# A two-part start, a moved weight queue and a re-made order for the first couples of an attention-plus-FFN kernel

## Chip, cores, metric

One core of one Trainium2 chip. The metric is the device time of one execution in microseconds (us). Every time below is from runs in the fast state unless it is called a single look. In single looks, which have one execution of each kernel, the state is unknown.

## The reference, cut to what matters

```python
q, k, v: float32 (8, 12, 448, 64)         # batch, heads, sequence, head dim
w_a, w_b: float64 (768, 1536); w_out: float64 (1536, 768)   # no astype: 8 bytes each
q_n = q / sqrt(mean(q*q) + 1e-6) * g_q     # the same for k
attn = softmax(q_n @ k_n.T / 8) @ v
x = attn.transpose(0, 2, 1, 3).reshape(3584, 768)
out = ((x @ w_a) * (x @ w_b)) @ w_out
```

Two things matter here. The q of a head must be squared, summed and rooted before its first score. And the weights arrive as 64-bit numbers (the "words" below), which the kernel has to fetch (1.5 MB for each of 18 pieces), round, combine into seven sums and store again ("kept") before the FFN can use them. That is done during the first twelve couples of the attention. A couple is four heads of one batch element; there are 24, numbered from 0.

## The kernel before

The kernel does not write its instructions in a fixed order. It describes them as operations with an engine, an estimated duration, a priority (a lower key goes first), what they read and write, and how many KB they load. `Plan.run` then simulates the engines and emits the operations in the order in which they would start. The emitted order is final: where ScalarE stood 3.51 us at a square in before's trace (86.13 us), the exponentials emitted behind it came after it (86.99 us), and TensorE waited 2.50 us for them.

```python
class Plan:
    TURN = 0.18
    LANES = 8
    RATE, LANDING = 300.0, 2.0      # belief: KB per us, and us from the last byte to usable
    LAG = 0.1                       # belief: from the end on one engine to the start on another
    ...
    def run(self):
        ...                         # the candidate that can start first, ties by key
                if ops[x][7]:       # a transfer: all of them share one modelled DMA
                    dma = max(dma, t) + ops[x][7] / self.RATE
                    end[x] = dma + self.LANDING
        ...
        for _, n in order:
            if ops[n][3] is not None:
                ops[n][3]()         # emitted in this order
```

The loads of q, k and v are issued by SyncE, one buffer each for q and k. The square is an operation of ScalarE, the sum of VectorE, the root of GpSimd:

```python
        def loads(p, nm):
            ...
            def emit():
                x = ld.tile(..., tag=nm, bufs=2 if nm == "v" else 1)
                for w in range(2):
                    nc.sync.dma_start(x[low_high[w]], pair.rearrange(...))
            op("SP", 0.8 if nm != "k" else 1.4, p - (1.8 if nm == "v" else 2.0), emit, [], [t], new=[t],
               kb=460 if nm != "k" else 800, dmas=2)
        ...
        def squares(s, nm):
                    nc.scalar.activation(t, flat, AF.Square)
                op("ACT", 1.07, key, square, [f"{nm}{p}"], [sq], new=[sq])
                op("DVE", 1.1, key, <sum of the squares>, [sq], [f"{ms}/{nm}"])
```

The words are issued by ScalarE, gated by how far the scores have come, and the rounded sums are stored from ScalarE's queue too:

```python
        LOADS = "ACT"
        KEEPS = "ACT"
        ...
                op(LOADS, 0.45, key - 0.75, load, after, [f"{row}/{part}"], kb=768)   # two per piece
        ...
            op(KEEPS, 0.45, key, keep, ..., kb=1376)
        ...
        GATES = [0, 2, 4, 4, 5, 5, 7, 7, 8, 8, 10, 10, 16, 18, 21, 21, 27, 32]
        seq = [15, 13, 16, 12, 14, 0, 1, 2, 3, 4, 5, 6, 7, 8, 9, 10, 11, 17]
```

The exponentials of the scores are ScalarE's as well. So one engine, in one fixed order, does the squares (which wait for loads), the exponentials (for which TensorE waits) and part of the rounding.

## Time and profile before

| | before |
|---|---|
| time, median of 4 runs | 1550.0 us (1547.28 to 1551.54) |
| span of the profiled execution | 1548.6 us |
| TensorE busy in it | 1506.9 us |
| TensorE idle: start and tail / first scores to 130 us / 130 to 250 / 250 to 1000 / later | 11.0 / 9.9 / 8.8 / 7.9 / 4.1 us |
| ScalarE waiting for q or k at a square, 13 to 245 us | 9.9 us |

The idle times are counted from the trace's matmul records; "start and tail" is what is left of span minus busy time. The three largest waits of TensorE over the whole run, in the view of who waited for whom (total us, times, longest):

```profile
PE sc L515 <- ACT ET L521: 10.6, 20, 1.3
PE o L537 <- ACT ET L521: 6.9, 8, 2.5
PE sc L515 <- ACT qkT L501: 6.0, 10, 1.2
```

All three are waits for ScalarE: twice for an exponential (ET), once for the copy of the transposed q (qkT). None is longer than 2.5 us. The start and the longest waits are shown in the prediction.

### The profile page before, as it was taken

What the parts mean: (1) busy time and instruction counts of PE and PEld (TensorE: products, weight loads), DVE (VectorE), ACT (ScalarE), POOL (GpSimd) and SP (SyncE); (2) the same over time, 40 slices, a digit from 0 to 9 for tenths busy, and PEclk for the clock granted to TensorE, in tenths of its full rate; (3) what the DMA queues carried; (4) which work ended last, traced back from release to release, by engine and by line L of the source; (5) the groups of instructions that cost most, each with busy time, mean ns of one, the idle gap of its engine ahead of it and who ended that gap; (6) DMA issues with size and microseconds to landing.
All of it is one profiled execution on the core that took longest, in us unless ns stands there. A gap on an engine that the chain in (4) does not pass through costs nothing.

```text
span 1548.6 us, 18051 instructions
## 1 busy us (share of the span) xinstructions
PE 1506.9 (97%) x6996; PEld 822.6 (53%) x6996; DVE 813.7 (53%) x1179; ACT 400.7 (26%) x654; POOL 314.1 (20%) x166
## 2 busy tenths in 40 slices
PE   8988999999999999999999999999999999999998
PEld 5553345555444555555444455555547855555796
DVE  5877869888786412222587543222237622222583
ACT  6767661111567100000445500000041000000000
POOL 3426432111345200011244300000111001000000
PEclk9999999999999999999999999999999999999999
DMA  9897445644445542212345456121226742222343
GB/s 269 240 268 199 97 108 178 218 163 175 143 118 128 150 146 76 103 71 107 102 110 152 114 159 199 72 107 71 95 83 206 247 159 100 79 82 91 111 140 110
DMA packets 128866, 214.74 MB, mean 139 GB/s; under 512 B 57860, under 2 KB 108292, under 8 KB 119044
## 3 DMA queue, kind: packets, MB, share of 16 engines
q1 hardware_dynamic: 100708, 160.02, 35.0%
q10 hardware_dynamic: 28064, 53.48, 9.9%
q8 instruction: 57, 0.93, 0.2%
q14 instruction: 37, 0.30, 0.1%
HBM read 169.08 MB, written 44.21 MB: 138 GB/s over the span
## 4 chain that ended last, share of the span: by engine, by line
PE 82%; DMA 7%; DVE 5%; ACT 3%; issue 1%; POOL 1%; SPq 1%; ACTq 0%; DVEq 0%; POOLq 0%
PE pq L1003 48%; PE po L726 16%; PE sc L515 5%; PE o L537 4%; DMA q_sb<-in_q_dram 2%; PE g L901 2%; PE a L901 2%; ACT ET L521 2%; PE pt L494 2%; DMA rec<-inv 1%; PE b L901 1%; PE su L573 1%; PE e L901 1%; PE d L901 1%; DMA lraw<-in_moe_w_b_dram 1%
## 5 line engine op out<-in xcount | busy, mean ns | idle before, releaser
L1003 PE MATMUL pq<-x,st 128*128 128x448 f32 x2016 | 763.5, 540 | 0.9 <-ACT rec L586 0.9
L1003 PEld LDWEIGHTS pq<-x,st 128*128 128x128 f32 x2016 | 381.2, 190 | 379.5 <-issue 371.2
L521 ACT ACTIVATE ET<-sc,ms 128x448 f32<-128x448 f32 x336 | 191.7, 633 | 92.2 <-PE sc L515 65.6
L515 PE MATMUL sc<-qkT 64*64 64x448 f32 x1344 | 177.2, 544 | 18.0 <-ACT ET L521 10.6
L537 PE MATMUL o<-ET,v_sb 64*64 64x448 f32 x1344 | 187.2, 545 | 7.5 <-ACT ET L521 6.9
L464 POOL TENSOR_TENSOR ms<-ms,expo 128x14 f32<-128x14 f32 x48 | 145.6, 3037 | 188.3 <-DVE ms L462 187.6
L1051 POOL TENSOR_TENSOR hT<-hT,t 128x448 f32<-128x448 f32 x24 | 28.4, 1185 | 744.7 <-DVE t L1049 742.5
L726 PE MATMUL po<-st,hT 128*128 128x384 f32 x504 | 166.4, 487 | 0.0
L726 PEld LDWEIGHTS po<-st,hT 128*128 128x128 f32 x504 | 95.0, 190 | 67.9 <-issue 3.9
L551 POOL TENSOR_TENSOR sum<-sum,ET 128x896 f32<-128x896 f32 x38 | 81.4, 2141 | 139.1 <-ACT ET L521 97.0
L1025 ACT COPY hT<-pq 128x448 f32<-128x448 f32 x24 | 12.8, 532 | 372.9 <-PE pq L1003 372.9
L515 PEld LDWEIGHTS sc<-qkT 64*64 64x64 f32 x1344 | 58.1, 132 | 95.2 <-issue 34.8
L537 PEld LDWEIGHTS o<-ET,v_sb 64*64 64x64 f32 x1344 | 60.2, 132 | 87.9 <-ACT ET L521 42.2
L726 PE MATMUL po<-st,fin 128*128 128x384 f32 x264 | 89.9, 490 | 0.0
L551 DVE TENSOR_TENSOR sum<-sum,ET 128x896 f32<-128x896 f32 x57 | 62.8, 1101 | 26.6 <-POOL sum L551 19.4
L726 PEld LDWEIGHTS po<-st,fin 128*128 128x128 f32 x264 | 49.1, 190 | 39.0 <-issue 7.0
L1063 POOL TENSOR_TENSOR hT<-hT,t 128x448 f32<-128x448 f32 x48 | 58.5, 1219 | 53.7 <-DVE t L1060 45.5
L458 DVE TENSOR_REDUCE ms<-sq 128x14 f32<-128x896 f32 x48 | 51.8, 1079 | 27.7 <-ACT sq L456 27.5
L1056 DVE TENSOR_TENSOR hT<-U,pq 128x448 f32<-128x448 f32 x48 | 29.8, 621 | 66.5 <-PE pq L1003 66.5
L746 DVE TENSOR_TENSOR o_sb<-fin,po 128x384 f32<-128x384 f32 x36 | 20.0, 554 | 80.2 <-PE po L726 72.4
L1060 DVE TENSOR_TENSOR t<-U,pq 128x448 f32<-128x448 f32 x48 | 29.7, 619 | 59.6 <-PE pq L1003 57.3
L1028 ACT COPY t<-pq 128x448 f32<-128x448 f32 x24 | 12.8, 533 | 176.0 <-PE pq L1003 176.0
(117 smaller groups left out, 1297.0 us busy)
## 6 DMA issues: line engine op xcount, KB each, us to landing
st<-kept SPq DMA_DIRECT2D x36, 1344.0 KB
st<-kept_o SPq DMA_DIRECT2D x28, 1152.0 KB
kept<-st ACTq DMA_DIRECT2D x12, 1344.0 KB
ti<-kept_t SPq DMA_DIRECT2D x48, 288.0 KB
q_sb<-in_q_dram SPq DMA_DIRECT2D x48, 224.0 KB
k_sb<-in_k_dram SPq DMA_DIRECT2D x48, 224.0 KB
v_sb<-in_v_dram SPq DMA_DIRECT2D x48, 224.0 KB
rec<-inv SPq DMA_DIRECT2D x48, 224.0 KB
```

The source lines that it names most:

```text
L458: op("DVE", 1.1, key, lambda: nc.vector.tensor_reduce(rs[p][:, s], xs["sq", nm, p], AX, ALU.add), [sq], [f"{ms}/{nm}"])
L464: lambda: nc.gpsimd.tensor_tensor(msf(), msf(), expo[:, 0:2 * NT * (b - a)], ALU.pow), [], names)
L494: nc.tensor.transpose(t[:, j * P:(j + 1) * P], x[:, j].rearrange("p h d -> p (h d)"), ident)
L515: nc.tensor.matmul(t[low_high[w], e, 0:S], lhsT=qkTs[p][low_high[e], 1, j * P + w * D:j * P + (w + 1) * D], rhs=qkTs[p][low_high[e], 0, w ...
L521: nc.scalar.activation(E[:, e], scs[p, j][:, e, 0:S], AF.Exp, scale=rs[p][:, 1, 2 * j + e:2 * j + e + 1])
L537: nc.tensor.matmul(os_[p][low_high[e], w, 0:S], lhsT=xs["v", p][low_high[w], e, j * D:(j + 1) * D], rhs=ETs[p, j][low_high[w], e], start=( ...
L551: two[e].tensor_tensor(sums[p], sums[p] if j > 1 else ETs[p, 0], ETs[p, j], ALU.add)
L726: nc.tensor.matmul(held["po"][:, 0:HALF], lhsT=a[0]()[:, c], rhs=sts[beta, 12 + place_of[f]][:, c], start=(c == 0), stop=(c == MH - 1))
L901: nc.tensor.matmul(held[bank], lhsT=x()[:, c], rhs=y(c), start=(start and c == 0), stop=(stop and c == MI - 1), skip_group_check=True)
L1003: nc.tensor.matmul(banks[bank][:, 0:S], lhsT=sts[at][:, f, c * P:(c + 1) * P], rhs=quads[x][:, c], start=(start and c == 0), stop=(stop an ...
L1056: take("DVE", 0.68, lambda bank=bank, i=i, n=n: V.tensor_tensor(C(i, n), held["U"], PS(bank), ALU.add), [f"p{ident_}.{bank}", U], [hp[i]])
L1063: lambda i=i, n=n, nm=nm: two[TIMES].tensor_tensor(C(i, n), C(i, n), held[nm], ALU.mult), [t], [hp[i]],
```

## The change

The intent: shorten the chain before the first scores by doing the first couple's q in two parts (four columns and three) and keep TensorE busy meanwhile with a sixth warm-up step; take the issues of the words off ScalarE; and let the plan make the order of the lead with other delays, meant to be closer to the chip's (the plan's belief, which no run here measures: a result reaches TensorE 0.22 us after it is done and the other engines after 0.05; DMA at 330 KB per us with 3 us landing). The core of the diff:

```diff
-    RATE, LANDING = 300.0, 2.0
-    LAG = 0.1
+    RATE, LANDING = 330.0, 3.0
+    LAG, LAG_PE = 0.05, 0.22
...
-        WARM = 5
+        WARM = 6
-        LOADS = "ACT"
+        LOADS = "SP"
-        ADD_UP = [None, 'DVE', 'POOL', 'DVE', 'POOL', 'DVE', 'DVE']
+        ADD_UP = [None, 'DVE', 'DVE', 'POOL', 'DVE', 'DVE', 'POOL']
...
-                op(LOADS, 0.45, key - 0.75, load, after, [f"{row}/{part}"], kb=768)
+                op(LOADS, 0.45, key - 0.25, load, after, [f"{row}/{part}"], kb=768)
...
+        FIRST = "q", 0
+        PARTS = slice(0, NT // 2 + 1), slice(NT // 2 + 1, NT)
+
+        def begin_first():            # second half of q 0, issued at once on ScalarE's queue
+            x = xs[FIRST] = ld.tile([P, 2, NT * D], FP32, tag="q", name="q_sb", bufs=1)
+            nc.scalar.dma_start(x[low_high[1]], q[0, 2:4].rearrange("h (p j) d -> p h (j d)", j=NT))
+
+        def prepare_first():          # square, sum, scale, root, product: each for c in range(2)
+            ...
+                op("ACT", 0.1 + 0.13 * n, key, square, ["q0"], [f"{sq}/{c}"], ...)
+                op("DVE", 0.1 + 0.145 * n, key, <sum>, [f"{sq}/{c}"], [f"{ms}/q{c}"])
+                op("POOL", 0.4 + 0.32 * n, key, <root>, [], [f"{ms}/q{c}"])
+                op("DVE", 0.1 + 0.145 * n, key, apply, [f"{ms}/q{c}", "q0"], [f"{qn}/{c}"], ...)
...                                    # k's roots, transposes and copy of q of couple 0: in two parts too
-            op("SP", 0.8, p - 0.0, spread_out, [t], [few], new=[few], kb=20, dmas=2)
+            op("SP", 0.8, p - 1.0, spread_out, [t], [few], new=[few], kb=20, dmas=2)
...                                    # the other three steps of the reciprocals likewise
-        GATES = [0, 2, 4, 4, 5, 5, 7, 7, 8, 8, 10, 10, 16, 18, 21, 21, 27, 32]
-        seq = [15, 13, 16, 12, 14, 0, 1, 2, 3, 4, 5, 6, 7, 8, 9, 10, 11, 17]
+        GATES = [0, 2, 5, 7, 10, 13, 14, 15, 19, 22, 24, 24, 26, 29, 30, 32, 40, 42]
+        seq = [12, 13, 15, 14, 16, 0, 1, 2, 3, 4, 5, 6, 7, 8, 9, 10, 11, 17]
-                    factors(n, x * 0.45 + 1.0, x < 2, [after])
+                    factors(n, x * 0.55 + 0.25, x < 1, [after])
```

No line of the diff orders the lead directly. The order comes out of the plan, so every constant above can move every instruction.

More of the change, by code (lines that the diff above doesn't have):

```diff
@@ L154, in run @@
                 for u in users.get(x, ()):
-                    ready[u] = max(ready[u], end[x] + (self.LAG if ops[u][0] != e else 0.0))
+                    ready[u] = max(ready[u], end[x] + ((self.LAG if e != "PE" else self.LAG_PE) if ops[u][0] != e else 0.0))
                     need[u] -= 1
@@ L429, in emit @@
             def emit():
-                x = ld.tile([P, NT, 2, D] if nm == "k" else [P, 2, NT * D], FP32, tag=nm, name=nm + "_sb", bufs=2 if nm == "v" else 1)
-                for w in range(2):
+                if (nm, p) == FIRST:
+                    x = xs.pop(FIRST)
+                else:
+                    x = ld.tile([P, NT, 2, D] if nm == "k" else [P, 2, NT * D], FP32, tag=nm, name=nm + "_sb", bufs=2 if nm == "v" else 1)
+                for w in range(1 if (nm, p) == FIRST else 2):
                     pair = src[b, h0 + 2 * w:h0 + 2 * w + 2]
@@ L435, in emit @@
                 xs[nm, p] = x
-            op("SP", 0.8 if nm != "k" else 1.4, p - (1.8 if nm == "v" else 2.0), emit, [], [t], new=[t],
-               kb=460 if nm != "k" else 800, dmas=2)
+            op("SP", 1.6 if (nm, p) == FIRST else 0.8 if nm != "k" else 1.4, p - (1.8 if nm == "v" else 2.0), emit, [], [t], new=[t],
+               kb=460 if nm != "k" else 800, dmas=1 if (nm, p) == FIRST else 2)
+        FIRST = "q", 0
[3 more added lines that the diff above has]
+            nc.scalar.dma_start(x[low_high[1]], q[0, 2:4].rearrange("h (p j) d -> p h (j d)", j=NT))
@@ new lines, in prepare_first, with begin, square, apply @@
+        def prepare_first():
+            ms, key, sq = tile_of("ms0", "ms", 3), -NORM, tile_of("sqq0", "sq", 1)
+            cut = lambda x, c: x.rearrange("p h (j d) -> p h j d", d=D)[:, :, PARTS[c]]
+            def begin():
+                rs[0] = wk.tile([P, 2, 2 * NT], FP32, tag="ms", name="ms", bufs=3)
+            op(None, 0.0, key, begin, [], [f"{ms}/q0", f"{ms}/q1", f"{ms}/k"], new=[ms])
+            qn = tile_of("qn0", "qn", 1)
+            for c in range(2):
+                n = PARTS[c].stop - PARTS[c].start
+                r = lambda c=c: rs[0][:, 0].rearrange("p (h j) -> p h j", j=NT)[:, :, PARTS[c]]
+                def square(c=c):
+                    if c == 0:
+                        xs["sq", "q", 0] = wk.tile([P, 2 * NT, D], FP32, tag="sq", name="sq")
+                    nc.scalar.activation(xs["sq", "q", 0].rearrange("p (h j) d -> p h j d", j=NT)[:, :, PARTS[c]], cut(xs[FIRST], c), AF.Square)
+                def apply(c=c, r=r, n=n):
+                    if c == 0:
+                        qns[0] = wk.tile([P, NT, 2, D], FP32, tag="qn", name="qn")
+                    nc.vector.tensor_tensor(
+                        qns[0].rearrange("p j h d -> p h j d")[:, :, PARTS[c]], cut(xs[FIRST], c),
+                        r().rearrange("p h j -> p h j ()").to_broadcast([P, 2, n, D]), ALU.mult)
+                op("ACT", 0.1 + 0.13 * n, key, square, ["q0"], [f"{sq}/{c}"], new=[sq] if c == 0 else [])
+                op("DVE", 0.1 + 0.145 * n, key, lambda c=c, r=r: nc.vector.tensor_reduce(
+                    r(), xs["sq", "q", 0].rearrange("p (h j) d -> p h j d", j=NT)[:, :, PARTS[c]], AX, ALU.add), [f"{sq}/{c}"], [f"{ms}/q{c}"])
+                op("DVE", 0.2, key, lambda r=r: nc.vector.tensor_scalar(r(), r(), 1.0 / D, 1e-6, ALU.mult, ALU.add), [], [f"{ms}/q{c}"])
+                op("POOL", 0.4 + 0.32 * n, key, lambda c=c, r=r, n=n: nc.gpsimd.tensor_tensor(
+                    r(), r(), expo[:, 0:2 * n].rearrange("p (h j) -> p h j", h=2), ALU.pow), [], [f"{ms}/q{c}"])
+                op("DVE", 0.1 + 0.145 * n, key, apply, [f"{ms}/q{c}", "q0"], [f"{qn}/{c}"], new=[qn] if c == 0 else [], lock=True)
@@ L439, in normalize @@
         def normalize(p):
-            ms, key = tile_of(f"ms{p}", "ms", 3), p - NORM
+            ms, key = f"ms{p}", p - NORM
             def begin():
                 rs[p] = wk.tile([P, 2, 2 * NT], FP32, tag="ms", name="ms", bufs=3)
-            op(None, 0.0, key, begin, [], [f"{ms}/q", f"{ms}/k"], new=[ms])
+            if p:
+                tile_of(ms, "ms", 3)
+                op(None, 0.0, key, begin, [], [f"{ms}/q", f"{ms}/k"], new=[ms])
+            else:
+                prepare_first()
@@ L472, in apply @@
                     ALU.mult)
-            squares(0, "q")
-            if p < APART:
-                roots(0, 1, [f"{ms}/q"])
+            if p:
+                squares(0, "q")
+                if p < APART:
+                    roots(0, 1, [f"{ms}/q"])
             squares(1, "k")
-            if p < APART:
+            if p == 0:
+                op("DVE", 0.2, key, lambda: nc.vector.tensor_scalar(rs[0][:, 1], rs[0][:, 1], 1.0 / D, 1e-6, ALU.mult, ALU.add), [],
+                   [f"{ms}/k", f"{ms}/k0", f"{ms}/k1"])
+                for c in range(2):
+                    r = lambda c=c: rs[0][:, 1, 2 * PARTS[c].start:2 * PARTS[c].stop]
+                    n = 2 * (PARTS[c].stop - PARTS[c].start)
+                    op("POOL", 0.4 + 0.16 * n, key, lambda r=r, n=n: nc.gpsimd.tensor_tensor(r(), r(), expo[:, 0:n], ALU.pow), [], [f"{ms}/k{c}"])
+            elif p < APART:
                 roots(1, 2, [f"{ms}/k"])
@@ L480, in normalize @@
                 roots(0, 2, [f"{ms}/q", f"{ms}/k"])
-            qn = tile_of(f"qn{p}", "qn", 1)
-            op("DVE", 1.15, key, apply, [f"{ms}/q", f"q{p}"], [qn], new=[qn], lock=True)
+            if p:
+                qn = tile_of(f"qn{p}", "qn", 1)
+                op("DVE", 1.15, key, apply, [f"{ms}/q", f"q{p}"], [qn], new=[qn], lock=True)
         def transposes(p):
@@ L503, in take, with turn_part, take_part @@
                                              AF.Copy, scale=gain[:, 0:1])
+                if (nm, p) == FIRST:
+                    for c in range(2):
+                        m = PARTS[c].stop - PARTS[c].start
+                        def turn_part(c=c):
+                            if c == 0:
+                                pts[0, 0] = ps_s.tile([P, 2 * 512], FP32, tag="sc", name="pt")
+                            for j in range(NT)[PARTS[c]]:
+                                nc.tensor.transpose(pts[0, 0][:, j * P:(j + 1) * P], qns[0][:, j].rearrange("p h d -> p (h d)"), ident)
+                        def take_part(c=c):
+                            nc.scalar.activation(qkTs[0][:, 0].rearrange("p (w j t) -> p w j t", w=2, j=NT)[:, :, PARTS[c]],
+                                                 pts[0, 0][:, 0:2 * S].rearrange("p (j w t) -> p w j t", w=2, j=NT)[:, :, PARTS[c]],
+                                                 AF.Copy, scale=gain[:, 0:1])
+                        op("PE", 0.11 * m, key, turn_part, [f"qn0/{c}"], [f"{pt}/{c}"], new=[pt] if c == 0 else [], mode="full")
+                        op("ACT", 0.1 + 0.145 * m, key, take_part, [f"{pt}/{c}", "gain"], [f"{qkT}/0"])
+                    continue
                 op("PE", 0.75, key, turn, [f"{nm}{p}" if n else f"qn{p}", f"half{p - 1}"], [pt], new=[pt], mode="full")
@@ L524, in scores @@
                mode="quad")
-            op("ACT", 1.12, p, exps, [sc, f"ms{p}/k"], [E], new=[E])
+            op("ACT", 1.12, p, exps, [sc, f"ms{p}/k" if p else f"ms0/k{int(j >= PARTS[1].start)}"], [E], new=[E])
         def values(p, j):
@@ L604, in invert @@
                 op("ACT", 0.55, p - 0.5, lambda w=w: move(w), [f"su{p}.{w}" if p < WIDE else f"su{p}"], [t], new=[t] if w == 0 else [])
-            op("SP", 0.8, p - 0.0, spread_out, [t], [few], new=[few], kb=20, dmas=2)
-            op("DVE", 0.3, p - 0.0, lambda: nc.vector.reciprocal(fews[0], fews[0]), [], [few])
-            op("SP", 0.4, p - 0.0, leave, [few], [f"inv{p}"], kb=20)
-            op("SP", 1.0, p - 0.0, come_back, [f"inv{p}"], [t], kb=460, dmas=2)
+            op("SP", 0.8, p - 1.0, spread_out, [t], [few], new=[few], kb=20, dmas=2)
+            op("DVE", 0.3, p - 1.0, lambda: nc.vector.reciprocal(fews[0], fews[0]), [], [few])
+            op("SP", 0.4, p - 1.0, leave, [few], [f"inv{p}"], kb=20)
+            op("SP", 1.0, p - 1.0, come_back, [f"inv{p}"], [t], kb=460, dmas=2)
         def quad(b, half):
@@ L1157, in fast_body @@
         with tc.manual_schedule():
+            begin_first()
             setup()
```

## The prediction

> **What bounds the kernel now.** I read the page first, then TensorE's busy time by stretches, then who TensorE waited for, then the first 16 us in order of time, and last the order of instructions of both programs on each engine.
>
> ```profile
> span 1548.6 us, 18051 instructions
> PE 1506.9 (97%) x6996; PEld 822.6 (53%) x6996; DVE 813.7 (53%) x1179; ACT 400.7 (26%) x654; POOL 314.1 (20%) x166
> ```
>
> TensorE is the bound: 1506.9 of 1548.6 us. The change takes no matrix product away (only the warm-up gains four), so all that it can win is TensorE's idle time, 1548.6 - 1506.9 = 41.7 us, and a part of its warm-up. Faster by 2% would need 31 us of these 41.7. The stretches say where the idle time lies (second column: length, then TensorE's busy time):
>
> ```profile
> 14.00:130.00 116.00, 106.09 (x1003) 63.66 (x999) 96.23 (x111) 83.95 (x129) 41.59 (x12) 1.00 0.95 265
> 130.00:245.00 115.00, 106.21 (x738) 46.71 (x731) 84.50 (x104) 72.29 (x117) 61.56 (x27) 1.00 0.51 132
> ```
>
> In the lead (the first twelve couples, up to 245 us) TensorE is idle for 9.9 + 8.8 = 18.7 us. Before 13.65 us it has no product of the attention at all. After 245 us some 16 us remain, over half of that in the last 450 us, at the products of the output and the last stores, whose order the change hardly touches. In the first stretch DMA is busy for 95%, VectorE for 83% and ScalarE for 72%, beside the time it spends issuing loads.
>
> The start, in order of time:
>
> ```profile
> 0.74 1.44 SPq L433 DMA_DIRECT2D q_sb<-in_q_dram  x2
> 1.36 5.66 PE L1094 MATMUL warm<-ident 128*128 128x128 f32 x32 [1.36 <-POOL ident masks.py:199]
> 5.30 0.95 ACT L456 ACTIVATE sq<-q_sb 128x896 f32<-128x896 f32 x1 [2.85 <-DMA q_sb<-in_q_dram]
> 6.28 1.08 DVE L458 TENSOR_REDUCE ms<-sq 128x14 f32<-128x896 f32 x1 [6.28 <-ACT sq L456]
> 7.73 5.15 POOL L464 TENSOR_TENSOR ms<-ms,expo 128x14 f32<-128x14 f32 x2 [6.27 <-DVE ms L462]
> ...
> 9.28 0.91 ACT L499 COPY qkT<-pt 128x896 f32<-128x896 f32 x1
> ...
> 10.36 1.09 DVE L468 TENSOR_TENSOR qn<-q_sb,ms 128x896 f32<-128x896 f32 x1 [0.18 <-DMA v_sb<-in_v_dram]
> 11.51 0.98 PE L494 MATMUL pt<-ident,qn 128*128 128x128 f32 x7 [1.24 <-DVE qn L468]
> 12.59 1.01 ACT L501 ACTIVATE qkT<-pt,gain 128x896 f32<-128x896 f32 x1 [2.40 <-PE pt L494]
> 13.65 1.73 PE L515 MATMUL sc<-qkT 64*64 64x448 f32 x16 [1.16 <-ACT qkT L501]
> ```
>
> It is one chain with nothing beside it: q lands at 5.30, then square, sum, root (half of 5.15), product, seven transposes, copy, and the first scores at 13.65: 8.35 us from the landing.
>
> Two of the waits in the lead:
>
> ```profile
> 74.10 1.73 PE L515 MATMUL sc<-qkT 64*64 64x448 f32 x16 [1.14 <-ACT qkT L501]
> 87.66 1.12 PE L537 MATMUL o<-ET,v_sb 64*64 64x448 f32 x5 [2.50 <-ACT ET L521]
> 86.13 0.95 ACT L456 ACTIVATE sq<-q_sb 128x896 f32<-128x896 f32 x1 [3.51 <-DMA q_sb<-in_q_dram]
> ```
>
> The first is a couple's boundary, where nothing stands between the transposes and the scores that need their copy: 1.14 us. The other two belong together: ScalarE stood 3.51 us at a square whose q had not landed, the exponentials behind it came late, and TensorE paid 2.50 us. This is an order made with a wrong idea of when q lands.
>
> [...] the warm-up's matmul records come at 6 to 7 per us until about 5 us and 10 per us after it. [...] in the trace the first transposes do start after all of the first 16 warm-up matmuls. [...] Here an issue of words costs ScalarE's queue 0.34 to 0.45 us, and DMA is near its limit in the first 130 us, so moving the words to the other queue should give ScalarE this time, not bandwidth.
>
> **The change, part by part.**
>
> 1. *q's second half is issued from ScalarE's queue.* The two issues of 1.44 us now stand beside each other, so the second starts some 0.75 us earlier, and k and the gains behind it too. I put q's landing at 4.6 and the gains' at 7.2 (before: 7.87).
>
> 2. *q in parts of four and three.* ScalarE's 448 elements take 532 ns and 896 take 951, so 0.11 + 0.94 per thousand: squares of 0.59 and 0.47. VectorE by the same reasoning: sums of 0.67 and 0.53, products of 0.68 and 0.55. A root of 14 took 2.57; I take 0.4 fixed: 1.64 and 1.33. Then: first sum 5.2 to 5.9, scaled at 6.1, second sum and its scaling to 6.8. In the new order VectorE does the gains next (0.35 + 0.21 + 0.14 and gaps), which land at 7.2: until 8.05. The roots run 6.15 to 7.8 and to 9.1. First product 8.1 to 8.8; then the sum of k (1.08) to 9.9; second product to 10.5. Three transposes with their drain to 11.15, copy of three columns to 11.75, scores at **11.8**. The other way into the scores is TensorE's own: its order is now 24 warm-up matmuls, gain, k's transposes, q's. The first 16 end at 7.0, eight more at 0.2 us each at 8.6; gain and k's transposes until 9.6; k's copy (0.91) to 10.55; the copies of q's two parts (0.59 + 0.47) to 11.75: the same 11.8. So the first scores come 13.65 - 11.8 = **1.85 us** earlier. The four added matmuls are paid beside q's chain.
>
> 3. *Words on the other queue.* Seven factors are loaded in the first 130 us, two issues each: 14 x 0.42 = 5.9 us that ScalarE's queue no longer spends. Only where it stood before an exponential that TensorE waited for does it count; I count it in the next part.
>
> 4. *The order of the lead.* I compared both orders of TensorE couple by couple. Boundaries where the scores follow the transposes directly: before at couples 3, 4, 5, after at 1, 2, 3, 5. One more, + 1.14 us. Against this stand the waits for exponentials: between 14 and 130 us the trace has 0.38 + 0.52 + 0.29 + 0.26 + 1.44 + 2.50 + 0.81 = 6.2 us. The larger ones come from squares and words that ScalarE takes too early; with later gates (fifth words after the tenth scores instead of the fifth) and no issues on its queue I expect about half to go: - 3.1. From 130 us the sums over keys hold one of two score banks until the reciprocal before them has come back, and the scores run at a step of 2.26 us with 0.53 idle. In the new order the sums stand later around couple 6 (seven scores after the transposes instead of two), the reciprocal's round trip has a higher priority, and 13 products of the FFN instead of 9 fill gaps ahead of the long run of it. Of the 8.8 us there I expect about a third back: - 2.9.
>
> Sum: - 1.85 + 1.14 - 3.1 - 2.9 = - 6.7. Past 245 us both orders differ in detail, with no direction that I can see; 0. From the median of 1550.15: 1543.4, rounded to **1543.5 us**.
>
> **Rivals.**
> - *The queue.* Words of 768 KB each now stand in the same queue as q, k and v, ahead of some of them. For it: landings of 9 us already occur in the lead and DMA is at 95%; a q behind 1.5 MB comes about 6 us later at 265 GB/s. Against it: the order is made knowing this, and the later gates spread the words. If it wins, ScalarE stands at squares as at 86 us, part 4 gives nothing or costs 3 us, and the time is 1548 to 1552.
> - *The start is bound otherwise.* The warm-up and k's copy, or the gains that VectorE waits for, set the first scores. I get the same 11.8 both ways, so a late gain or a slow warm-up gives at most 1 us away: 1544.5.
> - *The order is better than I credit.* All boundaries but these are covered and most of the 18.7 us go, 12 of them say: 1537.
> - *The wait moves.* An earlier start only makes couple 0 wait for the first words or v, and the 1.85 us are gone by couple 1: 1545.
>
> **Range and chances.** The ends come from the rivals: 1537 with the best order and 1549 with the queue taking the gain, while executions of the kernel before spread by 4 us. 8 in 10: 1537 to 1549. Faster by over 2% (under 1519) would need three quarters of all idle time: 0.01. Slower by over 2% needs 31 us of new waits: 0.01. Within 2%: 0.98.
>
> **What would show it.** First scores at 11.8 us (11.3 to 12.5), second product after the sum of k. TensorE's idle time from there to 245 us near 14 us instead of 18.7, with 1.1 us waits for the copy of q at couples 1, 2, 3 and 5, and waits for exponentials under 3.5 us up to 130 us. No issue of words on ScalarE's queue. After 245 us the same idle time within 1.5 us. I am wrong if ScalarE's waits for q's loads grow beyond the 7.6 us of the lead now, if the lead's idle time stays above 17 us, or if the gain lies after 245 us.

## The result, and the profile after

| | before | after |
|---|---|---|
| time, median of 4 runs each | 1550.0 us (1547.28 to 1551.54) | 1557.84 us (1557.17 to 1557.91) |
| span of the profiled execution | 1548.6 us | 1556.0 us |

The ratio after to before is 1.0053, 95% interval 1.0038 to 1.0068: slower by half a per cent, "same" at the 2% mark, and outside the predicted 1537 to 1549. Ratios here and below are the mean time of one kernel's fast runs over the mean of the other's in the same rounds, so not quite the ratio of the medians quoted.

The head of the page after:

```profile
span 1556.0 us, 18106 instructions
PE 1509.4 (97%) x7004; PEld 823.5 (53%) x7004; DVE 813.9 (52%) x1182; ACT 401.2 (26%) x656; POOL 316.0 (20%) x168
```

TensorE is still the bound. Of the 7.4 us between the two spans it was idle for 4.9 more and busy for 2.5 more:

| TensorE, us | before | after | difference |
|---|---|---|---|
| idle, start and tail | 11.0 | 9.6 | -1.4 |
| idle, first scores to 130 | 9.9 | 13.5 | +3.6 |
| idle, 130 to 250 | 8.8 | 13.4 | +4.6 |
| idle, 250 to 1000 | 7.9 | 6.7 | -1.2 |
| idle, after 1000 | 4.1 | 3.4 | -0.7 |
| busy | 1506.9 | 1509.4 | +2.5 |
| span | 1548.6 | 1556.0 | +7.4 |

So the loss lies in the lead, and the larger part past 130 us. Of the 2.5 us of busy time, 0.8 are the four added warm-up matmuls at 0.2 us; most of the rest is slower matmuls, as shown below. The same two stretches as in the prediction (length, then TensorE's busy time; the last three columns are granted clock, DMA share, GB/s):

```profile
14.00:130.00 116.00, 102.55 (x957) 60.86 (x948) 95.83 (x111) 80.06 (x123) 38.23 (x12) 1.00 0.91 261
130.00:245.00 115.00, 101.65 (x731) 43.69 (x730) 74.30 (x88) 71.89 (x117) 51.38 (x20) 0.97 0.44 106
```

The clock column of the second row is new: 0.97. Before it was 1.00 in both.

The waits of TensorE over the whole run, after:

```profile
PE o L609 <- ACT ET L593: 12.6, 7, 4.8
PE sc L587 <- ACT ET L593: 9.0, 16, 0.6
PE sc L587 <- ACT qkT L556: 6.3, 9, 1.9
```

Against before (6.9, 10.6, 6.0) the first row has almost doubled, with fewer waits (7 for 8) but a longest of 4.8 us instead of 2.5. A few large waits were added.

**The start.** The rows that answer to those of before:

```profile
0.74 0.75 ACTq L448 DMA_DIRECT2D q_sb<-in_q_dram  x1
1.36 7.12 PE L1166 MATMUL warm<-ident 128*128 128x128 f32 x48 [1.36 <-POOL ident masks.py:199]
5.43 1.04 ACT L465 ACTIVATE sq<-q_sb 128x512 f32<-128x512 f32 x2 [2.20 <-DMA q_sb<-in_q_dram]
8.46 0.35 DVE L246 SCALAR_TENSOR_TENSOR grow<-grow 1x64 f32<-1x64 f32 x2 [0.81 <-DMA grow<-in_g_k_dram]
9.20 0.69 DVE L470 TENSOR_TENSOR qn<-q_sb,ms 128x512 f32<-128x512 f32 x1
...
10.81 0.55 DVE L470 TENSOR_TENSOR qn<-q_sb,ms 128x384 f32<-128x384 f32 x1
...
11.81 0.55 PE L567 MATMUL pt<-ident,qn 128*128 128x128 f32 x3 [1.15 <-ACT qkT L570]
12.39 0.58 ACT L570 ACTIVATE qkT<-pt,gain 128x384 f32<-128x384 f32 x1 [0.64 <-PE pt L567]
13.03 1.74 PE L587 MATMUL sc<-qkT 64*64 64x448 f32 x16 [0.67 <-ACT qkT L570]
```

First scores at 13.03 instead of 13.65. The two issues of q do stand beside each other (0.74), and the second product does follow the sum of k. But q is usable only at 5.43 (before: 5.30), and VectorE stood 0.81 us for the gains until 8.46. The second three transposes then waited 1.15 us for ScalarE's copy of the first four; both parts share one PSUM tile. The 13.03 is also not what every execution gets. Six more profiles, of after_again and of experiments below, have this start and this order unchanged up to there: first scores at 12.76, 12.84, 13.59, 13.76, 13.80 and 13.86 us.

What was won at the start was gone by couple 1. ScalarE stood 2.59 us for the first words to be rounded, and TensorE waited behind it for an exponential of couple 0:

```profile
23.89 1.60 ACT L271 ACTIVATE st<-lraw 128x1536 f32<-128x1536 f32 x1 [2.59 <-DMA lraw<-in_moe_w_out_dram]
26.07 1.12 PE L609 MATMUL o<-ET,v_sb 64*64 64x448 f32 x5 [1.43 <-ACT ET L593]
```

This rounding starts at 23.39 to 24.09 us in all eight profiles that have this order of the lead and the words on SyncE's queue, whether their first scores came at 12.29 us or at 13.86. The four with first scores at 13.03 or earlier have such a wait (1.26 to 1.78 us); the four at 13.59 or later have none over 0.25 us there, but ran at half clock for 3.4 to 6.8 us from 12.0 to 14.2 us on. In all eight the first scores of couple 1 came at 34.56 to 35.20 us; in before's two profiles at 33.55 and 33.19.

**The large wait.** ScalarE, between 126 and 150 us in order of time:

```profile
140.36 0.95 ACT L502 ACTIVATE sq<-q_sb 128x896 f32<-128x896 f32 x1 [5.36 <-DMA q_sb<-in_q_dram]
141.22 2.19 ACT L593 ACTIVATE ET<-sc,ms 128x448 f32<-128x448 f32 x4
```

TensorE beside it:

```profile
136.14 0.93 PE L587 MATMUL sc<-qkT 64*64 64x448 f32 x8
141.89 2.29 PE L609 MATMUL o<-ET,v_sb 64*64 64x448 f32 x8 [4.82 <-ACT ET L593]
```

Three things are to be read here. ScalarE waited 5.36 us at the square of couple 7's q, with exponentials behind it whose scores were done. TensorE therefore waited 4.82 us. And then eight matmuls took 2.29 us where eight took 0.93 just before: half clock. The clock record of the trace is at 0.5 from 141.1 to 147.9 us, and the work from 141.89 to 147.9 costs some 3 us more by it (an estimate from 6.0 us of TensorE's busy time at clock 0.50). Before's clock record is at 1.0 from 5.2 us, within the warm-up, to 1544.6 us.

Why was q late? SyncE's queue, in order of time:

```profile
123.22 2.59 SPq L382 DMA_DIRECT2D lraw<-in_moe_w_b_dram  x2
125.92 3.07 SPq L436 DMA_DIRECT2D q_sb<-in_q_dram  x2
```

The q was issued directly behind two loads of words, 1.5 MB. Its packets (1,792 bytes) moved only from 134.7 to 139.3 us, and what the DMA engines did before that is in the DMA view of 130 to 134 us:

```profile
q10 hardware_dynamic: 125, 1.30, 77.1%
q1 hardware_dynamic: 368, 0.37, 27.1%
```

q10 is ScalarE's queue with the store of a kept piece (packets of 10.5 KB), q1 SyncE's with the words (1 KB packets); with the issues of the words, 28.1 MB went from q10 to q1 between the two pages. The store took 1.30 of 1.67 MB, the words got 0.37, and q stood behind the words. The square came 14.4 us after the first issue of this q began.

The order of TensorE for couples 5 and 6 shows why this hits. It reads K, Q transposes; s, o scores and values of one column; u sums; P a product of the FFN.

```
before  5: K Q s2 o1 s1 o1 s1 o1 s1 o1 s1 o1 s1 o1
        6: K P1 Q o1 s2 u1 o1 s1 o1 s1 o1 s1 o1 s1 o1 s1 o1
after   5: K Q s2 o1 s1 o1 s1 P1
        6: K Q o1 s1 o1 s1 o1 s1 o1 s1 o1 s2 o1 u1 o1 s1 o1 s1 o1 s1 o1 s1 o1
```

After, the transposes of couple 6 come when couple 5 is only half done, and ScalarE's order has the square of couple 7's q right behind them. The plan believed that it would have landed by then.

### The profile page after: what moved, and what is told of

Same layout as the page of the kernel before. It is cut to its first block, busy times and chain, and to the rows that moved or that the text cites. A ratio compares the mean times of both kernels' runs of the same rounds, so it can differ in the third digit from the quotient of the medians.

```text
span 1556.0 us, 18106 instructions
## 1 busy us (share of the span) xinstructions
PE 1509.4 (97%) x7004; PEld 823.5 (53%) x7004; DVE 813.9 (52%) x1182; ACT 401.2 (26%) x656; POOL 316.0 (20%) x168
## 3 DMA queue, kind: packets, MB, share of 16 engines
q1 hardware_dynamic: 121108, 188.11, 40.5%
## 4 chain that ended last, share of the span: by engine, by line
PE 86%; DMA 4%; DVE 4%; ACT 3%; issue 2%; POOL 1%; SPq 0%; ACTq 0%; DVEq 0%; POOLq 0%
PE pq L1075 47%; PE po L798 16%; PE sc L587 6%; PE o L609 6%; PE su L645 2%; PE g L973 2%; PE a L973 2%; PE pt L549 2%; ACT ET L593 1%; DMA k_sb<-in_k_dram 1%; DMA q_sb<-in_q_dram 1%; PE b L973 1%; PE e L973 1%; PE d L973 1%; DMA lraw<-in_moe_w_out_dram 1%
## 5 line engine op out<-in xcount | busy, mean ns | idle before, releaser
L609 PE MATMUL o<-ET,v_sb 64*64 64x448 f32 x1344 | 185.3, 550 | 13.8 <-ACT ET L593 12.6
L609 PEld LDWEIGHTS o<-ET,v_sb 64*64 64x64 f32 x1344 | 59.8, 133 | 91.6 <-ACT ET L593 43.0
```

Source lines behind the costliest of these rows:

```text
L609: nc.tensor.matmul(os_[p][low_high[e], w, 0:S], lhsT=xs["v", p][low_high[w], e, j * D:(j + 1) * D], rhs=ETs[p, j][low_high[w], e], start=( ...
```

## The experiments

All kernels gave correct results. In each session the kernel before ran on the same chip in the same rounds; its medians there were 1545.97, 1547.48, 1548.94 and 1547.18 us. The second of these sessions (the four kernels with an order made anew) lists the seven runs of the first and one more. Times of different sessions are therefore compared by their ratios. "Half clock" lists stretches of the trace's clock record at 0.5, from 10 to 245 us.

### q of couple 7 alone on the other queue

```diff
-  nc.sync.dma_start(x[low_high[w]], pair.rearrange(...))
+  (nc.scalar if (nm, p) == ("q", 7) else nc.sync).dma_start(x[low_high[w]], pair.rearrange(...))
```

The plan is not touched, so TensorE's order is the same as after.

> The changed kernel with one difference: q of couple 7 is issued from ScalarE's queue, so that it doesn't stand behind the words in SyncE's queue; TensorE's order is the same. Theory (the loss is one event: this q lands 5.36 us after ScalarE needs it, TensorE idles 4.82 us and then runs 6.8 us at half clock): ScalarE's wait for this q falls under 1 us, the stretch 137 to 148 us gets some 7.8 us shorter, no half clock there, time 1549.5 to 1551.5. Rival (the loss is spread over the lead by the new order, or the wait moves to the next load): time above 1555, idle moves to a neighbouring couple.

Measured: 1550.92 us (1548.87 to 1552.8), ratio 1.0014 [0.9987, 1.0041]. ScalarE's list around it:

```profile
125.42 1.36 ACTq L436 DMA_DIRECT2D q_sb<-in_q_dram  x2
...
136.00 1.05 ACT L556 ACTIVATE qkT<-pt,gain 128x896 f32<-128x896 f32 x1
136.90 0.99 ACT L502 ACTIVATE sq<-q_sb 128x896 f32<-128x896 f32 x1
```

The square follows the copy at once. From the transposes of couple 6 to those of couple 7 it is 23.26 us instead of 30.69, and there is no half clock there. TensorE's idle time from 130 to 250 us falls from 13.4 to 8.6 us. Moving two issues, 448 KB together, brought back 0.39% by the ratios (6.0 us; the two intervals just overlap). The medians differ by 6.9 us, but they are of two sessions. Of the kernels timed together with this one, the two that keep the late q, fill_gap and own_bank below, ran from 1553.09 us upwards, and this one up to 1552.8. The wait behind k of couple 4 stayed: 3.68 us at 91.69 (3.20 at 91.51 in after), here with 3.4 us of half clock behind it.

### The idle time filled, the late q kept

```diff
-  for w in range(2):
+  for w in [0, 1] * (6 if (p, j) == (5, 5) else 1):     # scores (5, 5), computed six times
```

> The changed kernel with one difference: the sixth scores of couple 5, the last work of TensorE before the 4.82 us of waiting, are computed six times over (same values), which keeps TensorE busy for 3.75 us of the wait. ScalarE's wait for q stays. Theory (the clock fell because of the idle time, and costs about 3 us by itself): no half clock between 140 and 150 us, time 1554.3 to 1555.3. Rival (the clock falls for another reason or costs nothing on the path): half clock stays, or time stays within 0.7 us of the changed kernel's 1557.8.

Measured: 1555.5 us (1553.09 to 1556.3), ratio 1.0044 [1.0017, 1.0072].

```profile
135.63 4.69 PE L587 MATMUL sc<-qkT 64*64 64x448 f32 x48
141.58 1.12 PE L609 MATMUL o<-ET,v_sb 64*64 64x448 f32 x5 [1.26 <-ACT ET L593]
```

ScalarE still waited 5.56 us for the q, but TensorE had work, and what came after it ran at full rate. The clock over 137 to 152 us, in the table by stretches, first after, then this kernel:

```profile
137.00:152.00 15.00, 9.47 (x68) 4.86 (x64) 5.87 (x8) 7.75 (x14) 6.21 (x4) 0.77 0.34 61
```

```profile
137.00:152.00 15.00, 12.90 (x128) 5.57 (x124) 8.94 (x10) 9.18 (x16) 7.37 (x4) 1.00 0.49 102
```

So the half clock there comes from the idleness. The gap between the transposes went from 30.69 to 28.19 us. (The 30.69 is the longest of the profiles with this wait: after_again and own_bank, with 3.4 us of half clock instead of 6.8, have 29.26 and 29.51. Against the 23.26 of q7_apart the late q so costs 6.0 to 7.4 us there.) The whole time does not show this clearly (1.0044 against 1.0053, intervals overlap), also because this execution fell to half clock at 14.2 and 82.4 us.

### All words back on ScalarE's queue, order of after

```diff
-  queue[LOADS].dma_start(...)      # LOADS stays "SP" in the plan
+  nc.scalar.dma_start(...)
```

> The changed kernel with the same orders on TensorE and VectorE, but every load of words issued from ScalarE's queue, at the place in the program where SyncE's queue had it. Theory (words in the queue of q and k delay those loads): ScalarE's waits for q and k in the lead fall from 15.9 us to under 8, no wait of TensorE over 3 us up to 245 us, no half clock, time 1548 to 1553. Rival (the order itself is the loss, whatever the queue): 1555 or more. Against the theory may work that ScalarE now issues the words and waits for their places.

Measured: 1569.37 us (1564.96 to 1571.17), ratio 1.0128 [1.0096, 1.0159]: slower than after. The waits of ScalarE from 13 to 245 us in this kernel:

```profile
ACT sq L502 <- DMA k_sb<-in_k_dram: 13.2, 3, 7.7
ACT sq L502 <- DMA q_sb<-in_q_dram: 7.6, 2, 3.8
```

20.8 us, against 15.9 after. With the words gone from SyncE's queue, ScalarE waited longer for q and k and not less. (ScalarE also issues the words here; no run separates the two.) "q and k share a queue with the words" is therefore no general cause; it holds for the one q of the first experiment. This theory was mine, and in the general form it fell. Half clock came five times here (22.3, 59.8, 87.1, 100.8, 145.2 us).

### The second part of the first transposes in its own PSUM tile

```diff
+  else:
+      pts[0, 2] = ps_mm.tile([P, 512], FP32, tag="mm", name="pt")     # part 1 of couple 0
```

> The changed kernel with the transposes of q's second part written to another PSUM tile than the first part's, so that they needn't wait until ScalarE has read the first part (1.15 us in the changed kernel). Theory (this wait took over half of what the start should give): transposes at 11.4 us instead of 11.8, first scores at 12.3 to 12.6 instead of 13.03 us, time 0.4 to 0.7 us lower, 1557.1 to 1557.5. Rival (k's copy on ScalarE binds anyway): first scores within 0.2 us of 13.03.

Measured: 1557.66 us (1556.09 to 1563.02), ratio 1.0073 [1.004, 1.0106]. First scores at 12.29 instead of 13.03, and the wait of 1.15 us for the copy is gone (0.75 for the product is left). That wait is explained, but nothing of it reached the time: TensorE waited 1.78 us at 26.24 us, behind words as shown above, and couple 1 had its first scores at 35.20 us (34.96 after). The wait at 141.29 us came again (4.91 us).

### One part of the change at a time, each with an order made anew

Four kernels, each the kernel before with some of the diff:

```diff
start_alone:      + two-part start, WARM 6;  words on ACT, old numbers for the order
queue_alone:      + LOADS = "SP";            all else as before
order_alone:      + RATE, LANDING, LAG, ADD_UP, keys, GATES, seq;  words on ACT, old start
order_and_queue:  + order_alone + LOADS = "SP";                    old start
```

> The kernel before with the start alone: q of couple 0 in two parts, its second half issued from ScalarE's queue, six warm-up steps; words stay on ScalarE's queue, all numbers of the order as before (the order is made anew from them). Theory (the loss lies in the order and queue of the lead): first scores near 13.0 instead of 13.65 us, no wait of TensorE over 3 us, ratio to the kernel before 0.998 to 1.001. Rival (any change shifts the made order and brings such an event): ratio over 1.003, with one wait of more than 3 us for exponentials.

> The kernel before with the words on SyncE's queue and nothing else changed. Theory now (a move of words between queues alone is not the loss, since moving them back cost another 11 us; what counts is which load stands ahead of which): ratio 0.998 to 1.004, ScalarE's waits for q and k up to 245 us between 8 and 14 us (before 9.9). Rival (the shared queue is the loss): ratio over 1.004 and ScalarE's waits for q and k over 14 us.

> The kernel before with the new numbers of the order (delays, landing, gates, order of the words, engine of the sums, priority of the reciprocals), words on ScalarE's queue, start as before. Theory (the new numbers make ScalarE take squares whose loads aren't there yet): ratio over 1.002, ScalarE's waits for q and k over 12 us up to 245 us. Rival (the order is good, only the queue spoils it): ratio below 0.999 and waits under 10 us.

> The changed kernel without its start: new numbers of the order and words on SyncE's queue, q of couple 0 whole, five warm-up steps. If the start has no part in the loss: ratio 1.004 to 1.009 (it loses the start's 0.6 us too) and again one long wait behind a load. If the loss is an accident of one made order: below 1.003, with no wait of TensorE over 3 us.

| kernel | median us | ratio [95%] | idle to 130 / 130 to 250 | largest waits of TensorE | half clock at |
|---|---|---|---|---|---|
| start_alone | 1556.78 | 1.0054 [1.0028, 1.0081] | 14.5 / 8.7 | 4.88 at 40.5 | 40.7, 95.3 |
| queue_alone | 1563.05 | 1.0094 [1.0067, 1.0121] | 12.5 / 13.2 | 3.87 at 114.7, 2.73 at 182.0 | 63.6, 114.8, 183.1 |
| order_alone | 1569.96 | 1.0139 [1.0113, 1.0165] | 14.1 / 17.0 | 4.73 at 143.0 | 12.4, 39.7, 87.5, 142.1 |
| order_and_queue | 1557.42 | 1.0061 [1.0035, 1.0087] | 13.6 / 11.1 | 3.54 at 113.9 | 13.3, 64.5 |

None is faster. In the ratio, start_alone and order_and_queue came as their less hopeful forecasts said. queue_alone missed: up to 1.004 was expected, though its waits for q and k (13.8 us) stayed within the forecast. Each re-made order has its own large waits in its own places. They are mostly for exponentials; two are for reciprocals (order_and_queue's 3.54 at a sum that waits for the reciprocal before it, and queue_alone's 2.73). The parts do not add up: order and queue together are less bad than either. In order_alone I had expected over 12 us of waits of ScalarE for q and k and there were 7.9, so its 1.4% is not told by those waits alone.

### The start within the old order

The kernel before with its own operations and numbers, so with the same order. The two parts are done inside the old operations; only the issue of q's second half moves:

```diff
 def first_square():        # in place of one square; sum, root, product and copy likewise
+    for c in range(2):
+        nc.scalar.activation(sq_(c), cut(xs["q", 0], c), AF.Square)
```

> The kernel before, its order kept to the last operation, with the start's parts written inside the same operations: q's second half issued from ScalarE's queue first, square, sum, root, product, transposes and copy each as four and three columns. Theory (the start is a small gain by itself, and start_alone lost only because the order was made anew): first scores at 12.6 to 13.0 instead of 13.65, ratio 0.998 to 1.000, no half clock. Rival (a start 0.8 us earlier shifts every load against its use and brings a late load and the half clock by itself): ratio 1.003 or more.

Measured in 5 rounds: 1551.04 us (1549.24 to 1554.08), ratio 1.001 [0.9996, 1.0023]. First scores came at 13.60, not at the expected 12.6 to 13.0: in the old order both products stand behind the sum of k (10.52), and the copy in two parts takes 1.16 us instead of 1.01. The half clock that was not expected came twice, at 86.4 and 137.6 us. So this run says that the replanned order, and not the splitting, costs start_alone most of its 0.5%; the sixth warm-up step, which it leaves out, is not tested apart. It does not say what an early start would gain.

### Two loads moved

The other repeated wait stood behind a k. I first moved the wrong one:

```diff
+  nc.scalar if (nm, p) in (("k", 5), ("q", 7)) else nc.sync        # two_apart
+  nc.scalar if (nm, p) in (("k", 4), ("q", 7)) else nc.sync        # k4_q7_apart
```

> The changed kernel with two loads on ScalarE's queue, q of couple 7 and k of couple 5 (the loads behind the two longest waits); TensorE's order is the same. Theory (the loss of the change is a few loads that land late for the place that the order gives their squares, plus the half clock after such waits): no wait of TensorE over 2 us between 85 and 150 us, no half clock there, 4 to 6 us below the run with q of couple 7 alone at its best, that is a ratio to the kernel before of 0.997 to 1.000. Rival (an earlier k only moves the wait to the next load): a new wait over 2 us within 30 us after 85 us, ratio 1.000 to 1.003.

> The same with the second part of q's transposes in its own PSUM tile. Theory: first scores at 12.3 to 12.6 us and 0.3 to 0.7 us below two_apart; rival: the start's gain is lost again at a later load, difference within 0.2 us or on the wrong side.

> The changed kernel with k of couple 4 and q of couple 7 issued from ScalarE's queue. (two_apart took k of couple 5; the k behind the wait of 3.2 us at 91 us of the changed kernel is that of couple 4, which the traces showed afterwards.) Theory (the loss is these two late loads and the half clock after them): no wait of TensorE over 2.2 us and no half clock from 80 to 150 us, ratio to the kernel before 0.996 to 0.999. Rival (the wait moves to another load): a new wait over 2.2 us in this stretch, ratio over 1.000.

k of couple 5 was not the late one; the load behind the wait at 91.5 us is k of couple 4. two_apart gave 1551.09 us (1550.72 to 1553.12), 1.0017 [1.0001, 1.0032], and by chance k of couple 4 was hardly late in its profile (0.95 us). Still a wait of 2.21 us at 124.77, with half clock, came in the stretch that was to have none. two_apart_own_bank, expected below two_apart with first scores at 12.3 to 12.6 us, had them at 12.90 and gave 1554.01 us (1551.13 to 1556.23), 1.0033 [1.0017, 1.0048], and there it was late again (3.35 us of TensorE at 91.79). Whether k of couple 4 lands in time thus differs between executions; that q of couple 7 lands late does not: with it in SyncE's queue behind the words and this order, it was late in all four executions looked at.

k4_q7_apart, with the right load, gave 1549.54 us (1547.39 to 1550.89), ratio 1.002 [1.0004, 1.0037]. ScalarE's waits for q and k in its lead are 5.0 us, down from 15.9. One wait of TensorE over 2.2 us is left:

```profile
79.36 3.14 PE L587 MATMUL sc<-qkT 64*64 64x448 f32 x16 [2.61 <-ACT qkT L556]
```

It is of my own making in part: the two issues of k take ScalarE 1.3 us just there. From 1.0053 to 1.002 is 0.33%, 5 us. This is no better than q7_apart with 1.0014, so moving k of couple 4 as well brought nothing that can be told. What the last 0.1 to 0.2% is, the runs do not settle. Two stretches of half clock are in this profile, behind that wait and at 14.0 us.

### The plan told that loads are slower

If the order is bad because the plan thinks loads are fast, a slower belief should mend it:

```diff
-  RATE, LANDING = 330.0, 3.0
+  RATE, LANDING = 250.0, 5.0     # slow_loads_250_5;  250, 4 and 200, 5 in the others
```

> The changed kernel with one line changed: the order is made with loads of 250 GB/s and 5 us of landing instead of 330 and 3. Theory (the order expects loads too early, so ScalarE is sent to squares whose q or k isn't there): ScalarE's waits for q and k up to 245 us under 8 us instead of 15.9, no half clock, ratio to the kernel before under 1.002. Rival (what any order brings is chance, whatever it believes of the loads): waits over 12 us or a half clock stretch, ratio 1.004 or more.

> The same with 250 GB/s and 4 us. Same theory and rival, with the same numbers; beside the run with 5 us it shows how much of a difference is chance of one made order.

> The same with 200 GB/s and 5 us. Theory: ScalarE's waits for q and k are smallest here, under 5 us, but later squares delay normalising, so that TensorE's waits for the copies of q grow; ratio 0.999 to 1.004. Rival: waits for loads as in the changed kernel, ratio over 1.004.

Measured: 1654.94 us (1.0695 [1.0677, 1.0713]), 1622.52 us (1.0489 [1.0472, 1.0507]) and 1704.36 us (1.1011 [1.0993, 1.103]). ScalarE's waits for q and k did vanish: 0, 0.2 and 0 us. But TensorE waited elsewhere; slow_loads_250_5, waits of the whole run:

```profile
PE su L645 <- ACT rec L658: 30.3, 3, 14.8
```

The kept pieces came late as well: 16.6 us of waits of the FFN's products for them, in two times. The belief also sets when the reciprocals' round trip through DRAM and the kept pieces are thought to be back, and the order made of it lets TensorE stand up to 14.8 us at a sum (17.4 in slow_loads_200_5). In the time, all three theories failed. None of the three slower figures makes a better order; that no single figure for all transfers could is argued, not shown.

### Both kernels once more

```diff
 before_again, after_again: no edit
```

> The kernel before, unchanged, for a second profile. Theory: the waits of TensorE for exponentials stay under 2.6 us, at the same places as in the first profile; the half clock may come behind the wait near 87 us (2.50 us in the first profile, without it) and would then cost under 2 us. Rival (the waits are chance from execution to execution, also in this kernel): a wait over 3 us at another place.

> The changed kernel, unchanged, for a second profile on this chip. Theory: the wait behind q of couple 7, 4.5 to 5.2 us near 142 us, and the half clock after it come back, since the order of the loads fixes them. Rival (it was chance of one execution): no wait over 3 us near 142 us.

Single looks: 1549.94 and 1554.83 us. After, the wait came again (4.57 us at 140.16) with half clock at 140.4. The start came out differently, too: the 24 warm-up matmuls (48 records) took 8.42 us instead of 7.12, and k's transposes waited for them until 10.02 (9.24 in the first profile):

```profile
1.36 8.42 PE L1166 MATMUL warm<-ident 128*128 128x128 f32 x48 [1.36 <-POOL ident masks.py:199]
```

First scores then came at 13.80, later than before's 13.65. The same is in fill_gap (8.47, scores at 13.86) and in k4_q7_apart (8.37, 13.76). Before's first 16 warm-up matmuls took 5.66 and 5.96 us in its two profiles, and there its k's transposes (7.93 and 7.95) are not held up.

The kernel before showed half clock too this time, at 87.8 us, behind a wait of 2.28 us (TensorE in order of time; note 1.51 us for the five matmuls, which took 1.12 in the first profile):

```profile
87.15 1.51 PE L537 MATMUL o<-ET,v_sb 64*64 64x448 f32 x5 [2.28 <-ACT ET L521]
```

## Why the prediction was wrong

It said 1543.5 us and a gain of 6.7; the spans show a loss of 7.4. By its own steps:

1. **q's second issue.** The issues stand beside each other as predicted, but q was usable at 5.43, not at 4.6. Issuing earlier did not land it earlier: in both traces q's packets begin at 2.27 to 2.28 us and the last ends at 4.36 (before) and 4.39 us (after), with k's beginning at 3.68 and 3.72. Why they did not move sooner stays open. The gains were ready for VectorE at 8.46, not 7.2.
2. **The two-part start: 0.62 us instead of 1.85.** The order of the steps was right; the first product came at 9.20, not 8.1, as the gains ahead of it did. The wait of 1.15 us for the shared PSUM tile was not in my sum at all; own_bank shows it: 12.29 without it. And "the four added matmuls are paid beside q's chain" fails in the executions where the warm-up takes 8.4 us: there TensorE's own way sets the first scores at 13.8, and the start gives nothing.
3. **Words off ScalarE's queue.** No issue of words is on it, as said.
4. **The order of the lead, 14 to 130 us.** The extra boundary came as said, at couples 1, 2, 3 and 5, at 1.14 us, one of them 1.90. The step that failed is "I expect about half to go: - 3.1". The waits for exponentials (1.43 + 0.25 + 1.21 + 0.88 + 3.20 + 0.78 = 7.75 against 6.2 us) grew, 3.20 of it behind k of couple 4.
5. **The order from 130 us: the step that failed most.** "About a third back: - 2.9" became 4.6 us more idle time and some 3 us of half clock. I had read TensorE's order there and counted sums and reciprocals. I had not asked where ScalarE's squares stand against the landing of their q. This one square (5.36 us) makes the difference: q7_apart, with the same order of TensorE, has 8.6 us of idle time there, as before has 8.8.
6. **After 245 us.** I said 0 within 1.5 us; from 250 us the idle time fell from 12.0 to 10.1, a little more than that.

Three readings in it are off, without weight in its sum. The warm-up's matmul records start 0.21 us apart until 5.15 us and 0.11 after, that is 4.7 and 9 per us; the 6 to 7 and 10 count those that reach into a stretch as well. TensorE's idle time after 245 us is 18.3 us and not "some 16". And in the new order six scores, not seven, follow couple 6's transposes before the sums.

**The rivals.** "The queue" had the mechanism: a q behind 1.5 MB of words in the same queue, and ScalarE at the square. I set it aside with "the order is made knowing this". The order was made with a belief, and for this load it was wrong. Its ceiling of 1552 was too low, as it had neither the size of the wait nor the half clock. It was wrong as a general statement, too, since words_act_queue is slower still. Of my signs for being wrong, idle time of the lead above 17 us came (26.9). Waits for q's loads beyond 7.6 us did not: they fell to 6.6, and it was the waits for k that grew, from 2.3 to 9.3. "The wait moves" came true in this order: couple 0 waits for the first words (1.43 us at 26.07, against 0.38 at 28.14 before), and the start's 0.62 us are gone by couple 1, whose first scores come 1.4 us later than before's. In the executions without this wait the start itself was late.

**What is shown and what is not.** Shown: the late q of couple 7 and its wait cost some 6 us (0.39% by the ratios, 6.0 to 7.4 us of the spacing of the transposes between traces). That in this order an earlier start is used up by couple 0's wait for words is read from eight profiles; no run tests it by itself. The half clock at 142 us comes from the idleness. The start within the old order costs nothing that can be told. Not settled: what each single constant of the new order does, for every edit to the plan brings another order with waits of its own; what an early start would be worth in the old order; and the last 0.1 to 0.2%. No version beat the kernel before.

## What to carry to other kernels

When a change re-makes an order, look for every instruction that waits for a transfer with work behind it on its engine (here ScalarE's square, 5.36 us, and the exponentials behind it), note what stands ahead of that transfer in its queue and which long waits would follow from a late landing; average waits and counts per couple did not show it. A TensorE wait of a few microseconds can cost twice, once as idle time and once as half clock after it (in after 4.82 us, then some 3 us by the estimate above). The earlier start here gained only as far as the next load that was already late (the first words, rounded from 23.39 to 24.09 us in eight profiles). Giving transfers of different kinds their own beliefs would be the next thing to try (untested here); measure a model-made order on the chip before trusting that better constants make a better order.

## What else the traces show

- Half clock also followed single waits of TensorE shorter than the 4.82 us in after: 2.28 us (before_again, 87 us), 2.53 and 1.83 us (start_same_order, 86.4 and 137.6 us). A wait of 2.50 us in before's first profile was not followed by it. What decides between them, no run tells.
- In 14 profiles of kernels with all warm-up steps in one row, 8 fell to half clock at 12.0 to 14.2 us, and in these the first two columns of scores took 2.96 to 3.27 us (3.00 in fill_gap) instead of 1.73 or 1.74. In 5 profiles of kernels that keep four warm-up matmuls between the transposes of k and of q, none did. No run tested this by itself. The 24 warm-up matmuls took 7.12 to 8.47 us from profile to profile. In after_again, fill_gap and k4_q7_apart they took 8.37 to 8.47 us, and the first scores came at 13.76 to 13.86 us, 0.7 to 1.1 us later than the 12.76 and 13.03 of q7_apart and after (7.15 and 7.12 us).
- Moving one q to the other queue took away a 5.36 us wait (q7_apart); the queue that it left held 1.5 MB ahead of it. The opposite move, all words to the other queue, made the waits for k and q longer (words_act_queue: 20.8 us against 15.9).
- The transposes of q's second part waited 1.15 us in after until ScalarE had copied the first part out of the same PSUM tile. With a tile of its own (own_bank) this wait was gone. Whether the program's guard of the whole tile or the hardware asks for it, no run tells.
